# FFN1 of two token blocks and two feature tiles by seven block products instead of eight, in a transformer block on one core

## The chip, the core and the metric

The kernel runs on one core of one Trainium2 chip. The metric is the device time of one execution in microseconds; before the change it is 1167.24 us, the median of 3 runs from 1166.67 to 1168.52. Engine names are those of the profile: PE multiplies matrices, DVE (vector) and ACT (scalar) work element by element, POOL does odd jobs, and SP issues nearly all transfers.

## The reference

One layer in which attention and a feed-forward network (FFN) read the same normalized input and both are added to it. There are 2048 tokens (S), width 576 (D), 32 heads of 18, and FFN width 4608 (F).

```python
xn = _layernorm(x, axis=-1)
return x + _A_ref(xn, A_wqkv, A_wo) + _B_ref(xn, B_w1, B_b1, B_w2, B_b2)
...
h = jnp.einsum("bsd,df->bsf", x, w1) + b1
r = jnp.where(h > zero, h, zero)
h = r * r
out = jnp.einsum("bsf,fd->bsd", h, w2) + b2
```

Attention is local: each token looks at itself and at 7 earlier ones, 2 apart.

## The kernel before

The tokens lie in four blocks (b) of 512, the FFN width in 36 tiles (f) of 128, and the 576 rows of width in 4 chunks of 128 and one of 64. Every fp32 operand is split into a high part (the fp32r rounding, written by ACT) and a rest (a subtraction on DVE), and a product is high x high + high x rest + rest x high. In the last chunk the 64 rows are doubled, so that high and rest share one matmul. So a step of FFN1 (`ffn1`, L448) takes 14 matmuls of 512 columns into one PSUM tile `wk`: 5 of high x high, 4 of the weights' high with `xl`, 5 of the weights' rest. Then ACT does relu with bias out of PSUM into `r`, and squares it twice, into the rounded `hh` and in place; DVE makes `hl`, the rest. FFN2 (`ffn2`, L486) of the step takes 14 matmuls more, onto five PSUM tiles `y` that stay open through a block.

The program walks through 4 x 36 = 144 such steps, `step(n)` at L618. Each step loads a tile of w1 (320 KB) and of w2 (288 KB), splits w1 for the next step (`split_w1`, one copy on ACT, one subtraction on DVE, 640 wide) and w2 for its own, and runs FFN2 two steps late (`LAG`). Between them stand, by a table of step numbers, the QKV projections of a block (4 groups of 8 heads, each 4 row tiles of 14 matmuls of 432 columns, `qkv_rows`), the attention of the groups on DVE, cut into pieces that a step takes three of (`piece`), the layernorm of the next block, and the output projection onto the same `y` tiles (`o_chunk`, `o_acc`). Only the first QKV group's order is written by hand (`open_rows`); else a scheduler sets each engine's order from the program's order and its own estimate of when things are ready. An engine then works through its list in that order.

In attention, DVE multiplies q with 8 shifted keys (`pr`, 1152 wide), sums up (`lg`), takes the softmax with one exponential on ACT, multiplies with the values and adds in three halvings, for each of 4 rows of queries. Keys and values of a group go to DRAM (`kscr`, `vscr`) and come back with the 14 tokens before them.

Of the kernel before, what the change touches and what calls it, by code (L numbers as in the profile page):

```python
# [2 lines left out]

# [17 lines left out]
NB = S // TB  # L21
NJ = TB // P
NC = 5
NF = F // P
G = 4
# [10 lines left out]
LAG = 2  # L36
WARM = 11
WQ, KV = 448, 2688
# [3 lines left out]
def block_kernel(ctx: ExitStack, tc: tile.TileContext, x, xt, wqkv, wo, w1, b1, w2, b2, out):  # L42
    nc = tc.nc
    const = ctx.enter_context(tc.tile_pool(name="const", bufs=1))
    mt = ctx.enter_context(tc.tile_pool(name="mt", bufs=1))
# [23 lines left out]
    nc.vector.tensor_reduce(out=flip[:, 0:1], in_=ident.rearrange("p (g f) -> p g f", g=G)[:, :, L // 2:],  # L69
                            axis=AX.XY, op=ALU.add)  # L70
    nc.vector.tensor_scalar(out=flip[:, 1:2], in0=flip[:, 0:1], scalar1=-2.0, scalar2=1.0, op0=ALU.mult, op1=ALU.add)
# [4 lines left out]
    vscr = [dram.tile([PAD + S, CG], F32, name=f"vscr{g}") for g in range(G)]  # L76

# [3 lines left out]

    oscr = {(b, g): dram.tile([TB, CG], F32, name=f"o{b}{g}") for b in range(NB) for g in range(G)}
    mrscr = {b: dram.tile([P, 2 * NJ], F32, name=f"mr{b}") for b in range(1, NB)}

    normed, mb = {0}, {}
    xb, xT, xr, xh, xl, qo, ob, wq = {}, {}, {}, {}, {}, {}, {}, {}
    raw1, raw2, w1s, w2s, hs = {}, {}, {}, {}, {}
    yp = {}

    def load_x(b):  # L90
        xb[b] = sb.tile([P, NJ, D], F32, name="xb", bufs=1)
        with tc.issue_after(last_load[0].ins):
            nc.sync.dma_start(xb[b], xv[b])
            xT[b] = sb.tile([P, NC, TB], F32, name="xt", bufs=1)
            nc.sync.dma_start(xT[b], xt[b])

    def load_first():
        xb[0] = sb.tile([P, NJ, D], F32, name="xb", bufs=1)
        raw = sb.tile([P, NC, TB], F32, name="xr", bufs=1)[:, :, :3 * CG]
        hi = mt.tile([P, NC, WQ], F32R, name="wqh")[:, :, :3 * CG]  # L100
        lo = mt.tile([P, NC, WQ], F32R, name="wql")[:, :, :3 * CG]
        nc.sync.dma_start(xb[0][:64, 0], xv[0, :64, 0])
        nc.scalar.dma_start(xb[0][64:, 0], xv[0, 64:, 0])
        nc.scalar.dma_start(raw[:, 0], wqkv[0, :, 0])
        nc.sync.dma_start(xb[0][:, 1], xv[0, :, 1])
        for c in range(1, NC):
            nc.sync.dma_start(raw[:, c], wqkv[0, :, c])
        for j in range(2, NJ):
            nc.sync.dma_start(xb[0][:, j], xv[0, :, j])
        for scr in (kscr[0], vscr[0]):  # L110
            nc.sync.dma_start(scr[:PAD], zero)
        return raw, hi, lo

    def split(hi, lo, raw, only=None):
        if only is not nc.vector:
            i = nc.scalar.activation(hi, raw, AF.Copy)  # L116
        if only is not nc.scalar:
            i = nc.vector.tensor_tensor(out=lo, in0=raw, in1=hi.bitcast(F32), op=ALU.subtract)  # L118
        return i

    def split_out(w, raw):
        nc.scalar.activation(w[:, :D], raw, AF.Copy)  # L122
        for o, a, n in ((NC * P, 0, DM), (D, DM, D - DM)):
            nc.vector.tensor_tensor(out=w[:, o:o + n], in0=raw[:, a:a + n], in1=w[:, a:a + n].bitcast(F32),  # L124
                                    op=ALU.subtract)

    ln, last_load, last_hl = {}, [None], [None]

    def open_x(b):
        xh[b] = mt.tile([P, NC, TB], F32R, name="xh", bufs=2)  # L130
        xl[b] = mt.tile([P, NC - 1, TB], F32R, name="xl", bufs=2)

    def bn_stats(b, j, k):
        if k == 0:
            ln[b, j] = sb.tile([P, 2, 6], F32, name="st", bufs=NJ)
        nc.vector.bn_stats(out=ln[b, j][:, k], in_=xb[b][:, j, k * 288:(k + 1) * 288])  # L136

    def mean_var(b, j):
        mv = sb.tile([P, 2], F32, name="mv", bufs=NJ)
        nc.vector.bn_aggr(out=mv, in_=ln[b, j])  # L140
        ln[b, j] = mv

    def inverse_std(rs, var):
        nc.vector.tensor_scalar(out=rs, in0=var, scalar1=EPS, scalar2=None, op0=ALU.add)  # L144
        nc.gpsimd.tensor_tensor(out=rs, in0=rs, in1=half, op=ALU.pow)  # L145

    def row_scale(j):
        mean_var(0, j)
        rs = sb.tile([P, 1], F32, name="rs", bufs=NJ)
        inverse_std(rs, ln[0, j][:, 1:2])  # L150
        return rs

    def minus_mean(j, rs):
        nm = sb.tile([P, 1], F32, name="nm", bufs=2)
        nc.vector.tensor_scalar(out=nm, in0=ln[0, j][:, 0:1], scalar1=-1.0, scalar2=rs, op0=ALU.mult, op1=ALU.mult)
        return nm

    def normalize_rows(xn, j, rs, on_act, nm=None):
        mv = ln[0, j]
        if on_act:  # L160
            nc.scalar.activation(xn[:, j, :D], xb[0][:, j], AF.Identity, bias=nm, scale=rs)
        else:
            nc.vector.tensor_scalar(out=xn[:, j, :D], in0=xb[0][:, j], scalar1=mv[:, 0:1], scalar2=rs,  # L163
                                    op0=ALU.subtract, op1=ALU.mult)
        nc.gpsimd.tensor_copy(xn[:, j, D:], xn[:, j, DM:D])

    def turn(y, xn, j, cs):
        for i, c in enumerate(cs):
            nc.tensor.transpose(y[:, i * P:(i + 1) * P], xn[:, j, c * P:(c + 1) * P], ident)  # L169

    def take(y, j, cs):
        js = slice(j * P, (j + 1) * P)
        if cs[0] < NC - 1:
            v = y[:, :len(cs) * P].rearrange("p (c t) -> p c t", c=len(cs))
            hi, lo = xh[0][:, cs[0]:cs[-1] + 1, js], xl[0][:, cs[0]:cs[-1] + 1, js]
            nc.scalar.activation(hi, v, AF.Copy)  # L176
            nc.vector.tensor_tensor(out=lo, in0=v, in1=hi.bitcast(F32), op=ALU.subtract)
        else:
            t = sb.tile([P, TB], F32R, name="r", bufs=3)[:, :P]
            hi = xh[0][:, NC - 1, js]  # L180
            nc.scalar.activation(t[64:], y[64:, :P], AF.Copy)
            nc.scalar.activation(hi[:64], y[:64, :P], AF.Copy)
            nc.vector.tensor_tensor(out=hi[64:], in0=y[64:, :P], in1=t[64:].bitcast(F32), op=ALU.subtract)

    def open_rows():
        xn = sb.tile([P, NJ, NC * P], F32, name="xt", bufs=1)
        open_x(0)
        y = open_y()
        raw, hi, lo = first_wq
        rs = {}  # L190

        def w_hi(c):
            nc.scalar.activation(hi[:, c], raw[:, c], AF.Copy)

        def w_lo(c, eng):
            eng.tensor_tensor(out=lo[:, c], in0=raw[:, c], in1=hi[:, c].bitcast(F32), op=ALU.subtract)  # L196

        def stats(j):
            for k in range(2):
                bn_stats(0, j, k)  # L200
            rs[j] = row_scale(j)
# [9 lines left out]
        def part(j, i):  # L211
            hi, lo = qw[0]
            a, c = divmod(i, 10)
            js = slice(j * P, (j + 1) * P)
            if (0, j) not in qp:
                qp[0, j] = pw.tile([P, TB], F32, name="wk")
                done[j] = 0
            done[j] += 1
            nc.tensor.matmul(qp[0, j][:, :3 * CG], (xl if a == 1 else xh)[0][:, c, js], (lo if a == 2 else hi)[:, c],  # L219
# [6 lines left out]
        done = {}  # L226
# [3 lines left out]
        normalize_rows(xn, 0, rs[0], False)  # L230
# [6 lines left out]
        nm = minus_mean(1, rs[1])  # L237
# [5 lines left out]
        normalize_rows(xn, 1, rs[1], True, nm)  # L243
        qkv_open(0, 0, (hi, lo))
# [5 lines left out]
        bn_stats(0, 2, 0)  # L250
        take(y[2], 0, (4,))
        bn_stats(0, 2, 1)
        rs[2] = row_scale(2)
# [5 lines left out]
        normalize_rows(xn, 2, rs[2], False)  # L259
        stats(3)  # L260
        nm = minus_mean(3, rs[3])
# [4 lines left out]
        qkv_out(0, 0, 0)  # L266
        normalize_rows(xn, 3, rs[3], True, nm)
        parts(1, 13, 4, 24)
        qkv_out(0, 0, 1)
# [3 lines left out]
        split_w1(0)  # L273
        parts(2, 12, 13, 4, 24)
        qkv_out(0, 0, 2)
        parts(3, 0, 1, 2, 3, 20, 21, 22, 23, 10, 11, 12, 13, 4, 24)
        split_w1(1)
        last_act = qkv_out(0, 0, 3)
        ffn1(0)
        qkv_close(0, 0)  # L280
        return last_act

    def layernorm(b):
        mr = sb.tile([P, 2, NJ], F32, name="mr", bufs=1)
        for j in range(NJ):
            for k in range(2):
                bn_stats(b, j, k)
            mean_var(b, j)
            nc.vector.tensor_copy(mr[:, 0, j:j + 1], ln[b, j][:, 0:1])
            inverse_std(mr[:, 1, j:j + 1], ln[b, j][:, 1:2])  # L290
            yield
        n = 2 * NJ
        nc.sync.dma_start(mrscr[b], mr.rearrange("p k j -> p (k j)"))
        mb[b] = sb.tile([P, P, 2, NJ], F32, name="mb", bufs=1)
        nc.sync.dma_start(mb[b].rearrange("c p k j -> c (p k j)"), flat(mrscr[b], 0, [0, P], n * P))

    def normalize(b):
        open_x(b)
        for c in range(NC):
            with tc.issue_after(last_hl[0].ins):  # L300
                for k, op in enumerate((ALU.subtract, ALU.mult)):
                    v = xT[b][:, c].rearrange("c (j p) -> c j p", j=NJ)
# [382 lines left out]
```

## Time and profile before

| | |
|---|---|
| median of 3 runs | 1167.24 us |
| span of the profiled execution | 1165.5 us |
| PE busy | 1157.4 us, 99% |
| DVE busy | 846.0 us, 73% |
| ACT busy | 602.0 us, 52% |
| granted clock of PE, mean | 0.998 |
| DMA | 185.90 MB, mean 160 GB/s |
| FFN1 matmuls (L460) | 2016 |
| FFN2 and projection matmuls (L483) | 2276 |

The span runs from the first to the last instruction of the profiled execution; the page gives it no other time. In a group's row stand the source line, the engine, what is written from what, the shape and the count; behind the bar the busy time of the group and the mean length of one in ns, and behind the second bar the engine's idle time just before such instructions with what ended it. Lengths of neighbours on an engine overlap a little. A matmul's length contains its way through the array; what counts is the distance between two. The chain of waits goes back from the last instruction to what released each; its pieces are given with start, length and count.

### The profile page before, as it was taken

What the parts mean: (1) busy time and instruction counts of PE and PEld (TensorE: products, weight loads), DVE (VectorE), ACT (ScalarE), POOL (GpSimd) and SP (SyncE); (2) the same over time, 40 slices, a digit from 0 to 9 for tenths busy, and PEclk for the clock granted to TensorE, in tenths of its full rate; (3) what the DMA queues carried; (4) which work ended last, traced back from release to release, by engine and by line L of the source; (5) the groups of instructions that cost most, each with busy time, mean ns of one, the idle gap of its engine ahead of it and who ended that gap; (6) DMA issues with size and microseconds to landing.
All of it is one profiled execution on the core that took longest, in us unless ns stands there. A gap on an engine that the chain in (4) does not pass through costs nothing.

```text
span 1165.5 us, 14768 instructions
## 1 busy us (share of the span) xinstructions
PE 1157.4 (99%) x5219; PEld 978.5 (84%) x5219; DVE 846.0 (73%) x1366; ACT 602.0 (52%) x1083; POOL 19.9 (2%) x33
## 2 busy tenths in 40 slices
PE   8999999999999999999999999999999999999998
PEld 6888888888888888888888888888888888888886
DVE  6868698892788686985287959698529795857452
ACT  6645445563545454555364545455535455445542
POOL 2001000000000100000000010000000000000000
PEclk9999999999999999999999999999999999999999
DMA  7656446332666556333266664534336745343321
GB/s 254 231 179 228 148 158 217 115 117 74 205 209 192 210 187 202 119 114 120 63 233 231 213 196 138 201 114 127 106 91 223 229 128 189 115 164 114 113 62 51
DMA packets 89114, 185.90 MB, mean 160 GB/s; under 512 B 9936, under 2 KB 36688, under 8 KB 87760
## 3 DMA queue, kind: packets, MB, share of 16 engines
q1 hardware_dynamic: 88816, 184.59, 48.6%
q8 instruction: 41, 0.67, 0.2%
q10 hardware_dynamic: 224, 0.37, 0.1%
q14 instruction: 33, 0.27, 0.1%
HBM read 165.96 MB, written 18.96 MB: 159 GB/s over the span
## 4 chain that ended last, share of the span: by engine, by line
PE 99%; DMA 0%; DVE 0%; POOL 0%; issue 0%; ACT 0%; POOLq 0%; DVEq 0%
PE y L483 44%; PE wk L460 39%; PE wk L340 14%; PE wk L219 1%; DMA xb<-in_x 0%; PE y L169 0%; DVE xt L163 0%; DVE st L136 0%; DVE xr L498 0%; POOL rs L145 0%; ACT xh L176 0%; DVE mv L140 0%; DVE rs L144 0%; DVEq L136 0%; POOLq L196 0%
## 5 line engine op out<-in xcount | busy, mean ns | idle before, releaser
L483 PE MATMUL y<-hh,w2s 128*128 128x512 f32 x1296 | 320.7, 389 | 0.0
L483 PEld LDWEIGHTS y<-hh,w2s 128*128 128x128 f32 x1296 | 243.3, 188 | 50.5
L460 PE MATMUL wk<-xh,w1h 128*128 128x512 f32 x720 | 210.2, 389 | 0.0
L483 PE MATMUL y<-hl,w2s 128*128 128x512 f32 x720 | 190.0, 389 | 0.0
L460 PE MATMUL wk<-xh,w1l 128*128 128x512 f32 x720 | 186.6, 389 | 0.0
L116 ACT ACTIVATE w1h<-raw 128x640 fp32r<-128x640 f32 x144 | 106.1, 737 | 118.0 <-PE wk L460 114.8
L118 DVE TENSOR_TENSOR w1l<-raw,w1h 128x640 fp32r<-128x640 f32 x144 | 117.9, 819 | 63.2 <-ACT w1h L116 46.1
L122 ACT ACTIVATE w2s<-raw 128x576 fp32r<-128x576 f32 x144 | 97.9, 683 | 119.8 <-PE y L483 119.0
L460 PEld LDWEIGHTS wk<-xh,w1l 128*128 128x128 f32 x720 | 135.2, 188 | 28.1
L483 PEld LDWEIGHTS y<-hl,w2s 128*128 128x128 f32 x720 | 135.2, 188 | 28.1
L460 PEld LDWEIGHTS wk<-xh,w1h 128*128 128x128 f32 x720 | 135.2, 188 | 27.0
L460 PE MATMUL wk<-xl,w1h 128*128 128x512 f32 x576 | 154.0, 389 | 0.0
L124 DVE TENSOR_TENSOR w2s<-raw,w2s 128x512 fp32r<-128x512 f32 (+1 forms) x288 | 118.1, 452 | 44.9 <-ACT w2s L122 43.9
L467 DVE TENSOR_TENSOR hl<-r,hh 128x512 fp32r<-128x512 f32 x144 | 98.7, 686 | 49.9 <-ACT r L466 49.9
L460 PEld LDWEIGHTS wk<-xl,w1h 128*128 128x128 f32 x576 | 108.1, 188 | 22.5
L462 ACT ACTIVATE r<-wk,b1t 128x512 f32<-128x512 f32 x144 | 98.5, 684 | 42.7 <-PE wk L460 42.5
L393 DVE TENSOR_TENSOR pr<-qo,kv 128x1152 f32<-128x1152 f32 x64 | 86.5, 1352 | 37.4 <-DMA kv<-kscr 37.4
L340 PE MATMUL wk<-wqh,xh 128*128 128x432 f32 x300 | 107.4, 358 | 0.0
L340 PE MATMUL wk<-wql,xh 128*128 128x432 f32 x300 | 107.4, 358 | 0.0
L466 ACT ACTIVATE r<-r 128x512 f32<-128x512 f32 x144 | 91.2, 633 | 4.4
L465 ACT ACTIVATE hh<-r 128x512 fp32r<-128x512 f32 x144 | 90.9, 632 | 4.3
L415 DVE TENSOR_TENSOR pr<-lg,kv 128x1152 f32<-128x1152 f32 x64 | 86.8, 1356 | 1.4
(83 smaller groups left out, 960.5 us busy)
## 6 DMA issues: line engine op xcount, KB each, us to landing
raw<-in_w SPq DMA_DIRECT2D x144, 320.0 KB, 3.1
raw<-in_w SPq DMA_DIRECT2D x144, 288.0 KB, 2.8
wqr<-in_wqkv SPq DMA_DIRECT2D x75, 216.0 KB, 3.4
kv<-kscr SPq DMA_DIRECT2D x16, 1008.0 KB, 5.8
kv<-vscr SPq DMA_DIRECT2D x16, 1008.0 KB, 8.4
raw<-in_wo SPq DMA_DIRECT2D x20, 288.0 KB, 2.7
kscr<-kv SPq DMA_DIRECT2D x16, 288.0 KB, 2.7
vscr<-kv SPq DMA_DIRECT2D x16, 288.0 KB, 3.2
```

The lines of the kernel that those rows point to most:

```text
L116: i = nc.scalar.activation(hi, raw, AF.Copy)
L118: i = nc.vector.tensor_tensor(out=lo, in0=raw, in1=hi.bitcast(F32), op=ALU.subtract)
L122: nc.scalar.activation(w[:, :D], raw, AF.Copy)
L124: nc.vector.tensor_tensor(out=w[:, o:o + n], in0=raw[:, a:a + n], in1=w[:, a:a + n].bitcast(F32), op=ALU.subtract)
L340: nc.tensor.matmul(ps, l, r, start=i == 0, stop=i == len(mm) - 1)
L415: nc.vector.tensor_tensor(out=pr.rearrange("p w (a d) -> p w a d", d=DH), in0=at[:, :, :, None].to_broadcast([P, W, HG, DH]), in1=shifted( ...
L460: nc.tensor.matmul(p, l, r, start=i == 0, stop=i == len(mm) - 1)
L462: nc.scalar.activation(r, p, AF.Relu, bias=b1t[:, f:f + 1])
L465: nc.scalar.activation(hh, r, AF.Square)
L466: nc.scalar.activation(r, r, AF.Square)
L467: last_hl[0] = nc.vector.tensor_tensor(out=hl, in0=r, in1=hh.bitcast(F32), op=ALU.subtract)
L483: nc.tensor.matmul(yp[b][c], v, a, start=first and c not in cs[:i], stop=last and c not in cs[i + 1:], skip_group_check=True)
```

## The change

The four blocks become two superblocks (s) of 1024 tokens, and the 36 feature tiles 18 pairs (q). For each of the 36 (s, q), a `quad` computes two feature tiles for two token blocks at once. The 512 full rows of width are halved, which makes the product a 2 x 2 by 2 x 2 block product; it is done by seven block products instead of eight, with sums of blocks prepared on both sides (Strassen's scheme in Winograd's form). A block product takes 6 matmuls of 512 columns: 2 chunks, each high x high, high x rest and rest x high. The last chunk of 64 rows goes on top of four of the products, 2 matmuls each. On the token side, `combine_x` prepares the sums `th`, `tl` once per superblock; on the weight side, `split_w1` makes four sums of 128x256 on DVE per quad and splits 2048 columns in two halves on ACT and DVE. Three PSUM tiles serve a quad, X, Y and V. X gathers products and is copied out three times between them by ACT (`snap`, with the bias); DVE adds these copies to Y and V (three adds of 128x512 out of PSUM per quad), and ACT takes the relu.

A superblock is done in two phases. In phase A, the quads run for both blocks; the relu of the first block (`r1`) is squared at once and goes to FFN2, one quad late, put into the quad's two gaps (`fill(0)`, `fill(1)`); the relu of the second block (`r2`) goes to DRAM (`rscr`, 512 KB a quad). In phase B it is loaded again, one q ahead, squared, and FFN2 of the second block runs; w2 is loaded and split again, as before once per block. Phase B of the first superblock also holds the QKV of the second's two blocks.

The start changes too: after the first QKV group, written by hand as before, all the other QKV groups of blocks 0 and 1 come first, and FFN1 starts after them. q goes through DRAM as keys and values do (`qscr`), and one wide copy on ACT per row tile replaces three. Attention is one stream over all 16 (block, group) that is drawn upon whenever the sum of DVE costs falls under 0.93 of PE's, both counted by a `Meter` from sizes as instructions are written. The buffers are fewer: w1 splits take 4 of 2048 columns, which the QKV weights share; raw w2 has 2 buffers for 3; and `r1`, `r2`, loaded relus, QKV results, residuals and projection inputs share 5 tiles of 1024 columns (`pair_tile`). As all calls go through `Meter`, most instructions of PE and DVE have line 57 in the changed kernel.

```diff
-    def ffn1(n):
-        b, f = divmod(n, NF)
-        hi, lo = w1s.pop(n)
-        p = pw.tile([P, TB], F32, name="wk")
...
-        for i, (l, r) in enumerate(mm):
-            nc.tensor.matmul(p, l, r, start=i == 0, stop=i == len(mm) - 1)
...
+    def split_w1(n):
+        r = raw1.pop(n)
+        hi = mt.tile([P, 2048], F32R, name="w1h", tag="w1", bufs=4)
+        lo = mt.tile([P, 2048], F32R, name="w1l", tag="w1", bufs=4)
+        part = lambda i: r[:, i * K2:(i + 1) * K2]
+        copy_hi(hi[:, :1024], r[:, K2:1280])
+        rest(lo[:, :1024], r[:, K2:1280], hi[:, :1024])
+        a21, a11, a12, a22 = (part(i) for i in range(4))
+        s1, s2, s3, s4 = (part(5 + i) for i in range(4))
+        vec.tensor_tensor(out=s1, in0=a21, in1=a22, op=ALU.add)
+        sub(s2, s1, a11)
+        sub(s3, a11, a21)
+        sub(s4, a12, s2)
+        copy_hi(hi[:, 1024:], r[:, 1280:])
+        rest(lo[:, 1024:], r[:, 1280:], hi[:, 1024:])
...
+    def squares(key, r):
+        hh = mt.tile([P, 2, TB], F32R, name="hh", bufs=2)
+        hl = mt.tile([P, 2, TB], F32R, name="hl", bufs=2)
+        nc.scalar.activation(hh, r, AF.Square)
+        nc.scalar.activation(r, r, AF.Square)
+        rest(hl, r, hh)
...
+        def product(p, i, first, extra=None):
+            o, bh, bl = ops[i]
+            mm = []
+            for k in range(2):
+                w = slice(o * K2 + k * P, o * K2 + (k + 1) * P)
+                mm += [(hi[:, w], bh[:, k]), (hi[:, w], bl[:, k]), (lo[:, w], bh[:, k])]
+            if extra is not None:
+                f, t = extra
+                w = slice(3 * K2 + f * P, 3 * K2 + (f + 1) * P)
+                mm += [(hi[:, w], xe[s][:, t]), (lo[:, w], xe[s][:, t])]
+            for j, (l, r) in enumerate(mm):
+                ten.matmul(p, l, r, start=first and j == 0, stop=j == len(mm) - 1, skip_group_check=True)
...
+        product(X, 1, True)
+        p1 = snap(X, 0)
...
+        product(Y, 2, True, (0, 0))
+        product(X, 6, False)
+        u2 = snap(X, 1)
+        add(r1[:, 0], Y, p1)
...
+        product(V, 7, True, (1, 1))
+        relu(r1[:, 0])
+        product(X, 5, False)
+        u4 = snap(X, 1)
+        add(r2[:, 1], V, u4)
+        fill(0)
+        relu(r2[:, 1])
+        product(X, 3, False, (0, 1))
+        nc.scalar.activation(r2[:, 0], X, AF.Relu, bias=bias[0])
+        nc.sync.dma_start(rscr[s, q], r2)
+        product(V, 4, False, (1, 2))
+        add(r1[:, 1], V, u2)
+        relu(r1[:, 1])
+        fill(1)
+        squares((b0, q), r1)
...
+    def load_r(s, q):
+        rp[s, q] = pair_tile("rs")
+        nc.sync.dma_start(rp[s, q], rscr[s, q])
...
+            squares((b, q), rp.pop((s, q)))
```

The order of PE in the middle of a superblock's work, FFN1 and FFN2 of block 0, where `wk` is FFN1's PSUM tile and `y` FFN2's. Before:

```order
L460 MATMUL wk<-xh,w1h 128x512 x4
L460 MATMUL wk<-xl,w1h 128x512 x4
L460 MATMUL wk<-xh,w1h 128x512
L460 MATMUL wk<-xh,w1l 128x512 x5
L483 MATMUL y_475<-hh,w2s 128x512
```

In the changed kernel, in the middle of phase A, a product of `th` with its tail of the last chunk (`xe`), and FFN2 behind it:

```order
L57 MATMUL wk<-th,w1h 128x512
L57 MATMUL wk<-tl,w1h 128x512
L57 MATMUL wk<-th,w1l 128x512
L57 MATMUL wk<-th,w1h 128x512
L57 MATMUL wk<-tl,w1h 128x512
L57 MATMUL wk<-th,w1l 128x512
L57 MATMUL wk<-xe,w1h 128x512
L57 MATMUL wk<-xe,w1l 128x512
L57 MATMUL y_1336<-hl,w2s 128x512
```

The 14 matmuls of a step in one run have become products of 6 or 8, and FFN2 stands between products.

The order of PE where the first QKV group ends. Before, FFN1 follows:

```order
L219 MATMUL wk<-wqh,xl 128x432 x4
L219 MATMUL wk<-wqh,xh 128x432
L219 MATMUL wk<-wql,xh 128x432
L460 MATMUL wk<-xh,w1h 128x512 x4
L460 MATMUL wk<-xl,w1h 128x512 x4
```

In the changed kernel, the next QKV group with newly split weights `wqh`, `wql` follows:

```order
L57 MATMUL wk<-wqh,xl 128x432 x4
L57 MATMUL wk<-wqh,xe 128x432
L57 MATMUL wk<-wql,xe 128x432
L57 MATMUL wk<-wqh,xh 128x432 x3
L57 MATMUL wk<-wql,xh 128x432
L57 MATMUL wk<-wqh,xl 128x432
```

The order of DVE among attention's instructions (`pr`, `lg`), with FFN's `hl` and the splits `w1l`, `w2s`. Before:

```order
L393 TENSOR_TENSOR pr<-qo,kv 128x1152
L467 TENSOR_TENSOR hl<-r,hh 128x512
L396 TENSOR_REDUCE lg<-pr 128x8x8
L124 TENSOR_TENSOR w2s<-raw_2642,w2s 128x512
L124 TENSOR_TENSOR w2s<-raw_2642,w2s 128x64
L393 TENSOR_TENSOR pr<-qo,kv 128x1152
L118 TENSOR_TENSOR w1l<-raw_2851,w1h 128x640
```

In the changed kernel, in the first phase A; `r_2658` and `r_2818` are `r1` of two quads that follow each other:

```order
L57 TENSOR_TENSOR pr<-q,k 128x1152
L57 TENSOR_TENSOR wos<-rwo,wos 128x512
L57 TENSOR_TENSOR wos<-rwo,wos 128x64
L57 TENSOR_TENSOR r_2658<-wk,snap 128x512
L57 TENSOR_REDUCE lg<-pr 128x8x8
L57 TENSOR_TENSOR w1l<-raw_2642,w1h 128x1024 x2
L57 TENSOR_TENSOR r_2818<-wk,snap 128x512
L57 TENSOR_TENSOR pr<-q,k 128x1152
L57 TENSOR_TENSOR hl<-r_2658,hh 128x1024
```

The adds out of PSUM, on which PE's next use of the tile waits, now stand in DVE's row between attention's instructions and the splits.

More of the change, by code (lines that the diff above doesn't have):

```diff
@@ L97, in load_first, with pair_tile @@
-    def load_first():
[L98 to L103, printed above, removed]
+    def pair_tile(name="rp"):
+        return mt.tile([P, 2, TB], F32, name=name, tag="r", bufs=5)
@@ new lines, in accumulate, with open_y @@
+    def accumulate(b, a_hi, a_lo, w, first, last, only=None):
+        ops = [o for o in w2_ops(a_hi, a_lo, w) if only in (None, o[0])]
+        cs = [o[0] for o in ops]
+        for i, (c, v, a) in enumerate(ops):
+            ten.matmul(yp[b][c], v, a, start=first and c not in cs[:i],
+                             stop=last and c not in cs[i + 1:], skip_group_check=True)
+    def open_y():
+        return [py.tile([P, TB], F32, name=f"y{i}") for i in range(NC)]
+    def squares(key, r):
[4 more added lines that the diff above has]
+        rest(hl, r, hh)
+        hs[key] = hh, hl
@@ L147, in row_scale @@
[L147 to L165, printed above, removed]
+        return rows, raw
@@ L642, in block_kernel @@
-    for n in range(NT + 1):
-        with opening() if n < 7 else ExitStack():
-            step(n)
+        nc.sync.dma_start(b1t, b1)
+        nc.sync.dma_start(b2t, b2)
+        side += [layernorm(1)]
+        for i, rows_of in enumerate(qkv_pass(0, (1, 2, 3), (1,), take_some)):
+            rows_of()
+            if i == 2:
+                drain_all(side)
+                load_xt(1)
+                side += [normalize(1)]
+            work(side)
+        drain_all(side)
+        spare[2:] = []
```

940 lines of the change are left out of this document (554 added, 386 removed).

## The prediction

> **What bounds the kernel now.** First the page's busy line, then its chain by engine, then the table of busy time by stage.
>
> ```profile
> PE 1157.4 (99%) x5219; PEld 978.5 (84%) x5219; DVE 846.0 (73%) x1366; ACT 602.0 (52%) x1083; POOL 19.9 (2%) x33
> PE 99%; DMA 0%; DVE 0%; POOL 0%; issue 0%; ACT 0%; POOLq 0%; DVEq 0%
> 0.00:30.00 30.00, 26.17 (x116) 20.35 (x117) 19.25 (x45) 19.31 (x46) 8.30 (x21) 0.94 0.77 258
> 300.00:600.00 300.00, 300.00 (x1355) 254.25 (x1354) 223.61 (x356) 156.20 (x281) 4.27 (x4) 1.00 0.51 169
> 600.00:900.00 300.00, 300.00 (x1355) 254.18 (x1355) 224.96 (x361) 156.64 (x279) 4.27 (x4) 1.00 0.50 163
> ```
>
> PE (first number after the stage's length) is busy 300.00 of 300.00 us at clock 1.00; DVE (third) stands at 75%. A busy PE need not be a full PE, so the chain's pieces give the pace, and its groups the counts.
>
> ```profile
> 23.57 8.43 PE wk L460 x37
> 74.38 10.97 PE wk L340 x56
> 1121.10 6.35 PE y L483 x28
> 1161.26 0.75 DVE L498 SCALAR_TENSOR_TENSOR xr<-y,b2t,xr 128x512 f32<-128x512 f32 x1 [0.29 <-PE y L483]
> L483 PE MATMUL y<-hh,w2s 128*128 128x512 f32 x1296 | 320.7, 389 | 0.0
> L483 PE MATMUL y<-hl,w2s 128*128 128x512 f32 x720 | 190.0, 389 | 0.0
> L483 PE MATMUL y<-kv,wos 128*128 128x512 f32 x260 | 62.8, 389 | 0.0
> L460 PE MATMUL wk<-xh,w1h 128*128 128x512 f32 x720 | 210.2, 389 | 0.0
> L460 PE MATMUL wk<-xh,w1l 128*128 128x512 f32 x720 | 186.6, 389 | 0.0
> L460 PE MATMUL wk<-xl,w1h 128*128 128x512 f32 x576 | 154.0, 389 | 0.0
> L340 PE MATMUL wk<-wqh,xh 128*128 128x432 f32 x300 | 107.4, 358 | 0.0
> L340 PE MATMUL wk<-wql,xh 128*128 128x432 f32 x300 | 107.4, 358 | 0.0
> L340 PE MATMUL wk<-wqh,xl 128*128 128x432 f32 x240 | 85.9, 358 | 0.0
> ```
>
> A 512-column matmul takes 6.35/28 = 0.2268 us, a 432-column one 10.97/56 = 0.1959. FFN1 has 720 + 720 + 576 = 2016, FFN2 and the output projection 1296 + 720 + 260 = 2276, QKV behind the opening 840. From 23.57: 23.57 + 840 x 0.1959 + 4292 x 0.2268 = 1161.5; the last drain starts at 1161.26. So PE has no gap at all after the opening, and every matmul taken out is worth 0.2268 us. Behind the last matmul lie 1165.5 - 1161.2 = 4.3 us. The span is 1.7 us under the median of 1167.2.
>
> **The matmuls.** A quad replaces 2 x 2 FFN1 steps of 14 matmuls, 56, by seven products of 6 and four tails of 2, 50. There are 36 quads: 1800 for 2016, 216 fewer, 216 x 0.2268 = 49.0 us. The order of PE keeps the counts of FFN2, projection and QKV. The stream alone then ends at 23.57 + 164.6 + 4076 x 0.2268 = 1112.6, the span at 1116.9, the median at 1118.6.
>
> [...]
>
> **What DVE gets.** Lengths of one instruction, with the releaser of idle time at the end of some rows:
>
> ```profile
> L118 DVE TENSOR_TENSOR w1l<-raw,w1h 128x640 fp32r<-128x640 f32 x144 | 117.9, 819 | 63.2 <-ACT w1h L116 46.1 <-PE wk L460 16.5 <-issue 0.3
> L467 DVE TENSOR_TENSOR hl<-r,hh 128x512 fp32r<-128x512 f32 x144 | 98.7, 686 | 49.9 <-ACT r L466 49.9
> L124 DVE TENSOR_TENSOR w2s<-raw,w2s 128x512 fp32r<-128x512 f32 x144 | 98.7, 686 | 44.9 <-ACT w2s L122 43.9
> L124 DVE TENSOR_TENSOR w2s<-raw,w2s 128x64 fp32r<-128x64 f32 x144 | 31.3, 218 | 0.0
> L415 DVE TENSOR_TENSOR pr<-lg,kv 128x1152 f32<-128x1152 f32 x64 | 86.8, 1356 | 1.4
> L393 DVE TENSOR_TENSOR pr<-qo,kv 128x1152 f32<-128x1152 f32 x64 | 86.5, 1352 | 37.4 <-DMA kv<-kscr 37.4
> L396 DVE TENSOR_REDUCE lg<-pr 128x64 f32<-128x1152 f32 x64 | 86.2, 1346 | 0.0
> L404 DVE TENSOR_TENSOR lg<-lg,mx 128x256 f32<-128x256 f32 x16 | 6.7, 419 | 0.2
> L501 DVE TENSOR_TENSOR xr<-y,xr 64x512 f32<-64x512 f32 x4 | 2.8, 694 | 0.1
> ```
>
> 512 and 1152 columns give 1.04 ns a column and 153 ns fixed, so 1024 columns take 1.22 us. Per quad: split of w1 2 x 1.22 + 4 x 0.419 = 4.11; three adds out of PSUM 3 x 0.694 = 2.08; hl 1.22; two w2 splits 2 x 0.904 = 1.81; together 9.2. Phase B repeats hl and w2: 3.0. That is 12.2 where four steps before took 4 x (0.819 + 0.686 + 0.904) = 9.6: 2.6 more per quad, 94 us in all. All of the changed kernel's DVE rows at such lengths come to 1014; before's come to 910 where the page has 846, since neighbours overlap. At that ratio, 0.93, DVE is busy 943 us, 84% of 1118. ACT falls: a 128x640 w1 copy per step becomes 2048 columns per quad for 2560.
>
> The mean hides the stages. One phase A quad is (50 + 28) x 0.2268 = 17.7 us of PE. From the first hl to the eighteenth, PE has 17 x 17.7 + 65 projection matmuls x 0.2268 = 315.5. DVE's order there holds 483 instructions, 340 us by length, of which 144 are attention (a (block, group) of it sums to 24.3) and 28 are rows of the next superblock's normalization that fill in; times 0.93, 316 with the filling and 290 without. In the second phase A, from the start to the eleventh hl, 224 x 0.93 = 208 against 209. So DVE has no room there beyond 25 us of work that nobody waits for. Phase B is easy: 200 x 0.93 = 185 us of DVE against 217 of PE, then 73 x 0.93 = 68 against 129.
>
> **Where PE may now wait.** ACT's lengths, and the loads that each stage needs:
>
> ```profile
> L116 ACT ACTIVATE w1h<-raw 128x640 fp32r<-128x640 f32 x144 | 106.1, 737 | 118.0 <-PE wk L460 114.8 <-DVE hl L467 1.4 <-DVE pr L393 1.4
> L462 ACT ACTIVATE r<-wk,b1t 128x512 f32<-128x512 f32 x144 | 98.5, 684 | 42.7 <-PE wk L460 42.5
> L466 ACT ACTIVATE r<-r 128x512 f32<-128x512 f32 x144 | 91.2, 633 | 4.4
> L116 ACT ACTIVATE wqh<-wqr 128x432 fp32r<-128x432 f32 x75 | 40.5, 561 | 84.7 <-DMA wqr<-in_wqkv 55.2 <-PE wk L340 29.2
> raw<-in_w SPq DMA_DIRECT2D x144, 288.0 KB, 2.8
> mb<-mr SPq DMA_DIRECT2D x3, 512.0 KB, 4.1
> kv<-vscr SPq DMA_DIRECT2D x16, 1008.0 KB, 8.4
> ```
>
> (1) Opening. FFN1 steps with ready weights follow the first QKV group today; now the next QKV group does, and its split stands on ACT behind the copy of the last row tile: about 0.6 + 0.56, then the matmuls run slower than the split. Between 0 and 4, taken 1.5.
>
> (2) Block 1's QKV starts 12 row tiles later, at 23.6 + 1.5 + 12 x 14 x 0.196 = 58, and needs xl of block 1. DVE's order has 55 us of lengths up to xl's second half, 51 at the ratio 0.93, and DVE idles 30 - 19.25 = 10.8 us of the first 30 today: 51 + 10.8 = 62. In that order eight attention instructions and three w2 splits stand ahead of the normalization. The reload of the statistics costs 4.1 by the row of mb, behind a store now made of 4-byte pieces. Between 0 and 10, taken 4.
>
> (3) The first quad has no FFN2 to cover its V: X's third product (8 x 0.227 = 1.8) covers snap and add (0.684 + 0.694) and little more. 0 to 3, taken 1.
>
> (4) A to B, twice: behind the last product stand add, relu, two squares of 1024 columns (about 1.05 each) and hl: 0.69 + 0.63 + 2.1 + 1.22 = 4.6 and five hand-overs; FFN2's 14 matmuls cover 3.2. Taken 2 each, 4; 0 to 8.
>
> (5) Adds, snaps and splits inside the other quads. Covers are 1.8 us for each snap and 14 to 34 matmuls (3.2 to 7.7) for the adds; an attention instruction ahead on DVE costs 1.35. With 25 us of slack DVE should hold. Taken 2; 0 to 15.
>
> The DRAM trip of the second block is hidden: a 512 KB load, 4.1 by mb's row, one FFN2 pair (28 x 0.2268 = 6.35) ahead; uncovered it would cost 4.1 once per phase. In bytes a phase B pair asks for 512 + 2 x 288 KB in 6.35 us, 175 GB/s, plus the next QKV; the first 30 us ran at 258. SP issues 36 stores and 36 loads more and 108 w1 loads fewer; POOL keeps its rows. Sum: 1.5 + 4 + 1 + 4 + 2 = 12.5; 1118.6 + 12.5 = 1131.1.
>
> **The rivals.** *DVE becomes the bound of phase A.* For: 316 of 315.5. Today each of 16 attentions waits 37.4/16 = 2.3 for its keys; if six and four such waits and an exponential's 0.4 each come unfilled, and the filling isn't put off, A loses 16 + 11 us: 1158. Against: 28 us can slip, and k is now loaded one half ahead.
>
> *The quad's serial chain, slower than before.* X is copied twice in mid-accumulation before PE may write on. Snap waits in ACT's order behind a relu that waits for a DVE add, itself behind two attention instructions: 2 x 1.35 + 0.694 + 0.684 - 1.8 = 2.3 us where it happens, against 1.1 (38/36) per quad from which the change loses. If every second of the 72 snaps in mid-accumulation meets it, 36 x 2.3 = 83: 1118.6 + 10.5 + 83 = 1212; if every third, 24 x 2.3 = 55: 1184. Against: PE's order pulls the next quad's first product in between.
>
> *Phase B starves.* raw2 has two buffers now, three before: split 0.68 + 0.90 and load 2.8 fit into 3.2 x 2 us, but at the 8.4 of vscr's load they don't: about 1 us in each of the 28 pairs without QKV, 1159.
>
> *Gaps cool the clock.* Row 0 to 30 has clock 0.94: 1.8 us lost beside its gaps. Five gaps at the hand-overs would cost 5 x 1.8: 1140. [...]
>
> That the change does not do what it says is excluded by the order: 1800.
>
> **How the numbers follow.** Forecast 0.68, DVE 0.12, chain 0.07, phase B 0.08, clock 0.05. All but the chain are faster; 0.2% is 2.3 us, which a measurement of this kernel just tells from none. Faster 0.91, same 0.02, slower 0.07. Low: no wait at all, 1118.6, less 1.6 for the run-to-run spread, 1117. High: the five terms' ends add to 40, 1159; not all meet, so 1158, where DVE's rival lies. The tails beyond hold the chain and half of phase B.
>
> **What would show it.** Right: 36 x 50 FFN1 matmuls at 0.227, PE idle near 12 us in the opening and at A to B, DVE near 940. Wrong: PE idle spread over the quads, released by DVE's adds (first rival) or ACT's snaps (second), by w2s in phase B, or a clock under 1.00 after 60 us; or a 512-column matmul that isn't 0.227.

## The result, and the profile after

The changed kernel takes 1185.08 us (median of 4 runs, 1179.87 to 1188.41), the one before 1167.49 (4 runs, 1166.67 to 1168.52): a ratio of 1.0145, 95% interval 1.0119 to 1.0172. It is slower, by 17.6 us, where 36 us less were forecast. The profiled execution took 1188.41, with a span of 1186.7; it is the longest of the four, so its losses below are some 3 us above those of the median.

From the changed kernel's page, the busy line, the chain by engine and the packets:

```profile
PE 1134.6 (96%) x5003; PEld 948.8 (80%) x5003; DVE 922.0 (78%) x1458; ACT 584.0 (49%) x837; POOL 17.6 (1%) x33
PE 66%; DVE 16%; DMA 13%; issue 2%; ACT 2%; SPq 1%; POOL 0%; DVEq 0%; ACTq 0%; POOLq 0%
DMA packets 88918, 214.46 MB, mean 181 GB/s; under 512 B 13072, under 2 KB 36752, under 8 KB 84368
```

The 216 matmuls are gone (5003 for 5219), and DVE is at 922 us, under the 943 forecast. But the chain, 99% PE before, now has 29% of DVE and DMA in it. The table by stage says where. After a stage's length come the busy time in us and the instructions of PE, PEld, DVE, ACT and POOL, then the granted clock, the share of DMA and its GB/s:

```profile
30.00:75.00 45.00, 38.61 (x183) 35.87 (x182) 33.05 (x49) 16.87 (x29) 1.07 (x2) 0.92 0.94 251
75.00:140.00 65.00, 62.64 (x301) 56.16 (x300) 58.90 (x88) 30.94 (x50) 0.00 (x0) 1.00 0.53 178
140.00:225.00 85.00, 85.00 (x376) 70.38 (x376) 79.97 (x122) 46.95 (x64) 0.00 (x0) 1.00 0.52 181
225.00:300.00 75.00, 64.33 (x261) 51.64 (x261) 54.72 (x112) 31.92 (x45) 6.25 (x8) 0.91 0.64 143
300.00:420.00 120.00, 119.56 (x528) 98.66 (x527) 113.48 (x178) 63.10 (x89) 0.00 (x0) 1.00 0.53 175
420.00:520.00 100.00, 93.39 (x405) 76.39 (x404) 86.84 (x126) 56.87 (x80) 0.00 (x0) 0.98 0.67 225
520.00:1005.00 485.00, 483.44 (x2184) 409.79 (x2184) 396.50 (x606) 243.58 (x348) 0.00 (x0) 1.00 0.54 180
1005.00:1100.00 95.00, 80.82 (x311) 64.08 (x310) 39.80 (x66) 37.49 (x48) 0.00 (x0) 0.89 0.43 140
```

In the middle of phase A (140 to 225) PE does 376 matmuls in 85.00 us, 0.226 each: the stream is as forecast. Most of the loss sits in four places: 30 to 75, 225 to 300, 420 to 520 and 1005 to 1100. In the last, 95 us would hold 419 matmuls; 311 are done, 108 or 24.5 us fewer. PE is idle for 95 - 80.82 = 14.2 of that; the other 10 are matmuls at a clock of 0.89. In this trace the granted clock is 1 or 0.5 and never between; a stretch at 0.5 is called a spell below.

The same for the whole trace: from each matmul's start to the next, less 0.2268 (0.1959 for 432 columns), distances over by more than 0.3 us counted as waits, the rest as slow matmuls. (A matmul's length in the rows of before, 389 ns for 512 columns and 358 for 432, is 162 ns over its distance in both.)

| place, us | term of the forecast | waits | slow matmuls |
|---|---|---|---|
| 24 | (1), 1.5 | 1.4 | |
| 30 to 75 | (2), 4 | 7.0 | 2.6 |
| 75 to 140 | (3), 1 | 2.7 | 0.4 |
| 225 to 300 | none | 11.5 | 4.6 |
| 420 to 520 | (4), 2 | 7.6 | 2.5 |
| 300 to 420, 520 to 1005 | (5), 2 | 2.5 | 0.5 |
| 1005 to 1030 | (4), 2 | 2.0 | 1.7 |
| 1030 to 1100 | none | 13.9 | 7.1 |

Together 68.0; the span less the gapless one is 1186.7 - 1116.9 = 69.8, and the 1.8 left over lie in the opening.

What PE waited for, the four largest rows of the table of waits (total, times, longest):

```profile
PE y L57 <- ACT wos L115: 12.9, 6, 4.5
PE wk L57 <- DVE r L57: 9.5, 4, 4.2
PE y L57 <- DVE hl L57: 6.4, 2, 6.2
PE wk L57 <- ACT qkv L249: 6.4, 2, 5.0
```

No row says that DVE is the bound of a whole phase, and ACT's `snap` has 1.1 us in two waits. The wait of 5.0 us in the last row begins at 54 us. ACT stood for 11.5 us at the split of w2, until its load landed at 58, with QKV's copies queued behind it. The DMA view of 40 to 58 us (slices of 0.45 us, busy tenths and GB/s; then loads, KB and us to landing):

```profile
DMA  9998699999999929999199536359687999979999
GB/s 438 438 392 276 205 348 394 410 371 382 292 170 182 231 10 20 20 13 10 3 10 15 5 10 10 10 20 44 31 46 54 161 261 300 310 295 392 390 366 256
wqr<-in_wqkv SPq DMA_DIRECT2D x1, 432.0 KB, 12.2
raw<-in_w SPq DMA_DIRECT2D x1, 288.0 KB, 11.0
```

From the fifteenth slice on, for 7.6 us, the queues move 3 to 54 GB/s, and yet are busy for more than half of the time. Under way is the 4 KB store of block 1's statistics, in 1024 pieces of 4 bytes, issued at 36 and landed 19.1 us later. The w2 load issued meanwhile takes 11.0 us, where the median before was 2.8. The page counts 13072 packets under 512 B for 9936 before, 3136 more; three stores of 1024 pieces, where there were 128 pieces each, are 2688 of them. The two other stores, issued at 239 and 265, lie in front of the waits that begin at 246 and 277.

The waits from 1030 on are another thing. The chain there:

```profile
1041.89 0.69 ACT wos L115
1042.63 9.00 PE y L57 x28
1051.65 0.70 ACT w2s L115
1052.37 3.54 DMA rwo<-in_wo
1055.99 0.69 ACT wos L115
1056.73 8.27 PE y L57 x28
```

A ring: the split of w2 frees a raw buffer, only then wo is loaded into it, split, and used; its split tile frees the next. The output projection's `rwo` and `wos` share the two raw and three split tiles of w2 (`o_chunk`).

At the entry of phase B (466 us) PE waits 3.43 us for the last quad's add, which stands in DVE's order behind this:

```profile
464.69 0.82 DVE L57 TENSOR_TENSOR w2s<-raw,w2s 128x512 fp32r<-128x512 f32 x2
465.43 1.22 DVE L57 TENSOR_TENSOR xraw<-xraw 128x1024 f32<-128x1024 f32 x1
466.57 1.35 DVE L57 TENSOR_TENSOR pr<-lg,v 128x1152 f32<-128x1152 f32 x1
467.84 1.22 DVE L57 TENSOR_TENSOR xraw<-xraw 128x1024 f32<-128x1024 f32 x1
468.97 0.68 DVE L57 TENSOR_TENSOR r<-wk,snap 128x512 f32<-128x512 f32 x1
```

For 30 us around this hand-over DVE (third) has hardly a gap:

```profile
450.00:480.00 30.00, 25.34 (x107) 20.80 (x106) 29.94 (x41) 17.71 (x28) 0.00 (x0) 0.94 0.64 214
```

So there were four theories: (1) the 4-byte store jams the queues; (2) the projection's ring of shared tiles; (3) the normalization of the next superblock, ahead of the last quad's add; (4) a wait of PE brings a spell. The rival to the first three is that DVE, or the two raw buffers alone, make the waits.

### The profile page after: what moved, and what is told of

It reads as the page before. It is cut to its first block, busy times and chain, and to the rows that moved or that the text cites. A ratio compares the mean times of both kernels' runs of the same rounds, so it can differ in the third digit from the quotient of the medians.

```text
span 1186.7 us, 14078 instructions
## 1 busy us (share of the span) xinstructions
PE 1134.6 (96%) x5003; PEld 948.8 (80%) x5003; DVE 922.0 (78%) x1458; ACT 584.0 (49%) x837; POOL 17.6 (1%) x33
## 2 busy tenths in 40 slices
DMA packets 88918, 214.46 MB, mean 181 GB/s; under 512 B 13072, under 2 KB 36752, under 8 KB 84368
## 4 chain that ended last, share of the span: by engine, by line
PE 66%; DVE 16%; DMA 13%; issue 2%; ACT 2%; SPq 1%; POOL 0%; DVEq 0%; ACTq 0%; POOLq 0%
PE y L57 35%; PE wk L57 31%; DMA raw<-in_w 4%; DVE pr L57 3%; DMA rwo<-in_wo 2%; DVE xraw L57 2%; DVE lg L57 1%; DMA wqr<-in_wqkv 1%; DVE wql L57 1%; DMA o<-q 1%; DVE hl L57 1%; DMA xb<-in_x 1%; DVE w2s L57 1%; DMA mr<-mr 1%; DMA kscr<-qkv 1%
## 5 line engine op out<-in xcount | busy, mean ns | idle before, releaser
L57 PE MATMUL wk<-th,w1h 128*128 128x512 f32 x288 | 112.5, 391 | 4.5 <-DVE r L57 4.5
L57 PE MATMUL wk<-tl,w1h 128*128 128x512 f32 x288 | 112.5, 391 | 0.0
L57 PE MATMUL wk<-th,w1l 128*128 128x512 f32 x288 | 112.2, 390 | 0.0
L57 DVE TENSOR_TENSOR r<-wk,snap 128x512 f32<-128x512 f32 x108 | 73.8, 683 | 42.6 <-PE wk L57 25.7
L57 PE MATMUL wk<-wqh,xl 128*128 128x432 f32 x256 | 92.4, 366 | 0.0
L57 DVE TENSOR_TENSOR pr<-q,k 128x1152 f32<-128x1152 f32 x64 | 86.5, 1352 | 2.3 <-DMA k<-kscr 1.6
L57 DVE TENSOR_TENSOR pr<-lg,v 128x1152 f32<-128x1152 f32 x64 | 86.6, 1353 | 0.9
L57 DVE TENSOR_TENSOR w1l<-raw,w1h 128x1024 fp32r<-128x1024 f32 x72 | 86.6, 1217 | 0.9 <-ACT w1h L115 0.9
L57 PE MATMUL wk<-xh,w1h 128*128 128x512 f32 x216 | 84.4, 391 | 2.7 <-DVE r L57 1.6
L57 DVE TENSOR_REDUCE lg<-pr 128x64 f32<-128x1152 f32 x64 | 86.2, 1348 | 0.5
L57 PE MATMUL y<-oh,wos 128*128 128x512 f32 x260 | 72.4, 424 | 13.9 <-ACT wos L115 12.9
```

The source lines that it names most:

```text
L57: return f(*args, **kw)
```

## The experiments

All are edits of the changed kernel but the fourth, which edits the kernel before. The third joins the first and the second, the sixth the fifth and the second; the seventh builds on the sixth, the ninth on the seventh, the tenth on the ninth. Ratios are to the kernel before. The scheduler sets the orders anew for each kernel. By the traces, the fourth has the order of the kernel before on every engine, and the second and the eighth have that of the changed kernel up to 1009 us; in the first, the fifth, the seventh, the ninth and the tenth other instructions moved too, so there the edit is not the only difference.

**The store in 32-byte pieces.** The layout of before, one piece per partition, read with a stride:

```diff
-        nc.sync.dma_start(mrscr[b].rearrange("n p -> p n"), mr.rearrange("p k j -> p (k j)"))
+        nc.sync.dma_start(mrscr[b], mr.rearrange("p k j -> p (k j)"))
...
+                    vec.tensor_tensor(out=u, in0=u, in1=rows[:, k], op=op)
```

> Edit: the changed kernel, in which alone the store of the layernorm statistics goes back to one piece of 32 bytes per partition (as before the change), and the normalization reads them with a stride instead. Theory 1 (the 3 stores of 1024 pieces of 4 bytes jam the queues: the w2 and w1 loads issued meanwhile take 10 to 15 us): the store lands within 4 us, the waits of PE at 54, 67, 246 and 277 us and the half-clock spells behind them go (5.3 + 1.7 + 2.3 and 16 us), and the time comes to 1160 (1155 to 1167). Rival (DVE at its limit, or the two raw buffers of w2 by themselves make these waits): the waits stay, 1185 +- 4.

Measured: 1181.5 us, 1.0121 (1.0101 to 1.014). A miss of 21.5 us, and the store of block 1 still took 9.7 us to land where 4 were expected. The stage tables show the theory at work in one place: at 225 to 300 the loss falls from 16.1 to 3.7. At 30 to 75 it is 8.4 for 9.6, and at 420 to 520 it grows from 10.1 to 22.9:

```profile
225.00:300.00 75.00, 73.13 (x316) 60.02 (x316) 67.58 (x131) 39.39 (x55) 7.86 (x8) 0.98 0.55 175
420.00:520.00 100.00, 86.31 (x348) 69.81 (x347) 82.38 (x119) 51.06 (x72) 0.00 (x0) 0.91 0.57 184
```

The edit had a price of its own. This kernel's normalization reads its statistics 8 words apart; below it is a contiguous row of twice the columns (min, median, max ns), and then the same step in the kernel before the change, where it was read so too:

```profile
L57 DVE TENSOR_TENSOR xraw<-xraw,mb x24: 1056/1129/1203, 53.7 to 445.3; 128x512 f32<-128x512 f32 x24
L57 DVE TENSOR_TENSOR xraw<-xraw x8: 1160/1220/1252, 64.9 to 462.9; 128x1024 f32<-128x1024 f32 x8
```

```profile
L303 DVE TENSOR_TENSOR xt<-xt,mb x30: 1122/1147/1183, 233.7 to 803.3; 128x512 f32<-128x512 f32 x30
```

1.129 us where half of 1.220 would do: 24 x 0.52 = 12 us more on DVE, 16 of the 24 (8 us) between 420 and 446, ahead of the hand-over at which DVE is full. So the edit changed two things, and it shows what transposing the statistics had bought.

**Own tiles for the last projection.** In the last block `th` and `w1` are idle:

```diff
+        else:
+            r = mt.tile([P, 2 * TB], F32, name="rwo", tag="th", bufs=4)[:, :D]
+            w = mt.tile([P, 2048], F32R, name="wos", tag="w1", bufs=4)[:, :2 * D]
```

> Edit: the changed kernel, in which alone the output projection of the last block gets other buffers: raw wo from the idle th tiles (4) and the split wo from the idle w1 tiles (4), instead of sharing 2 raw buffers and 3 split buffers with w2. Theory 2 (load, split and use of wo and w2 stand in one serial ring): the six waits of 2.2 to 4.8 us between 1020 and 1095 us and the half-clock spells behind them go, 18 to 25 us, and the time comes to 1163 (1159 to 1168). Rival (the load itself, or DVE's transposes of the attention output, is what comes late): the waits stay and the time is 1185 +- 4.

Measured: 1167.46 us, 1.0004 (0.9992 to 1.0016), 17.6 less. All but one of the waits go:

```profile
1005.00:1100.00 95.00, 92.97 (x402) 76.03 (x401) 47.30 (x82) 46.06 (x61) 0.00 (x0) 0.98 0.56 176
```

402 matmuls for 311, and the loss is 4.2 for 24.7. Theory 2 stands: nothing moved ahead of 1009 us, and the five waits on `wos` are gone. The wait of 2.2 us at the start of the stage, the second hand-over from A to B, stays.

This run, with the eighth, also tells how far a stage differs between two profiles of one order. At 75 to 140 us, where the changed kernel has 301 matmuls, the second and the eighth have:

```profile
75.00:140.00 65.00, 59.49 (x277) 53.31 (x276) 54.41 (x80) 28.47 (x47) 0.00 (x0) 0.95 0.51 168
75.00:140.00 65.00, 64.22 (x310) 57.92 (x309) 59.08 (x87) 31.87 (x51) 0.00 (x0) 1.00 0.53 178
```

The loss there is 3.1, 8.5 and 1.1 us with no edit near: one wait for a quad's add is 1.6 us, 4.7 or none.

**Both.**

> Edit: both edits of the first two experiments at once. If the two causes stand apart in time and share nothing, the gains add: 1138 (1132 to 1146), with PE's waits left at the entry of phase B of the first superblock (10 us with cold matmuls), in the opening and at the first quads. If instead DVE is the bound behind them, time gained in one place is lost in another: 1155 or more.

Measured: 1163.5 us, 0.9956 (0.9933 to 0.9978). The two gains were 3.6 and 17.6, together 21.2; 21.6 came. They add as far as these 7 runs, from 1157.5 to 1168.0, can tell, but with one gain of 3.6 that is a weak test; the miss is that of the first experiment.

**The store alone, in the kernel before.** The other way round:

```diff
-        nc.sync.dma_start(mrscr[b], mr.rearrange("p k j -> p (k j)"))
+        nc.sync.dma_start(mrscr[b].rearrange("n p -> p n"), mr.rearrange("p k j -> p (k j)"))
```

> Edit: the kernel before the change, in which alone the statistics are stored transposed, in 4-byte pieces, as in the changed kernel. Theory 1: the store's landing grows from 1.4 to 12 us or more each time, and the loads issued in that time take about 11 us for 3; with three raw buffers and no shared ring PE loses between 0 and 15 us, so 1167 to 1182. Rival (the piece size is harmless and the store was slow in the changed kernel because of what else was queued): it lands within 5 us and the time is 1167 +- 2.

Measured: 1182.08 us, 1.0123 (1.0108 to 1.0138): 14.7 us lost by three stores of 4 KB, with the order of every engine as before, with another FFN1, other buffers and DVE at 73%, and although the normalization gets its contiguous rows. The time is at the end of the range; the stores landed after 9.4, 10.4 and 8.8 us, for 2.8, 1.4 and 1.4 before, where 12 or more were expected. Its DMA view from 88 to 108 us (slices of 0.5 us), and what PE waits for:

```profile
DMA  1000979899999959562959236357039799999989
GB/s 61 20 0 0 138 226 406 336 369 239 281 126 114 32 81 97 32 48 16 65 16 65 16 16 32 16 32 65 0 97 339 300 409 395 439 374 487 453 356 432
raw<-in_w SPq DMA_DIRECT2D x1, 320.0 KB, 13.9
raw<-in_w SPq DMA_DIRECT2D x1, 288.0 KB, 10.2
mr<-mr SPq DMA_DIRECT2D x1, 4.0 KB, 9.4
```

```profile
PE wk L460 <- DVE w1l L118: 7.7, 3, 3.1
PE wk L460 <- ACT w1h L116: 3.7, 2, 2.2
```

For 8 us the queues carry 97 GB/s at most, a load of w1 takes 13.9, and PE waits 1.7 us for its split at 106.

The other two stores, at 394 and 689, cost more, and in another way. SP issues in order, and the reload of the statistics waits for their store to land. Behind the reload stand the loads of the next attention, of QKV's weights and of w1. SP's wait there (total, times, longest), in the kernel before and in this run, and the DMA view of 689 to 697 us (slices of 0.2 us):

```profile
SPq L295 <- DMA mr<-mr: 2.0, 2, 1.0
SPq L295 <- DMA mr<-mr: 24.7, 3, 10.0
```

```profile
DMA  0001776000000000000000000000000000000000
GB/s 0 0 0 1 7 7 6 0 0 0 0 0 0 0 0 0 0 0 0 0 0 0 0 0 0 0 0 0 0 0 0 0 0 0 0 0 0 0 0 0
mr<-mr SPq DMA_DIRECT2D x1, 4.0 KB, 8.8
```

Nothing else is under way: the pieces pass within 0.8 us, and the store lands 7 us later, at 697.6. Only then are the reload and all behind it issued: the load of w1 is issued 21.1 us behind the store, 11.9 before. PE's other four waits, 9.7 of the 11.4 us, begin at 417, 421, 711 and 716. So late landing is shown to be the cause in this kernel; that it jams other loads is seen at the first store alone.

**The store in 128-byte pieces, read contiguously.** The clean form of the first:

```diff
+        vec.transpose(turned, rows8)
+        for i in range(P // L):
+            nc.sync.dma_start(mrscr[b][:, i * L:(i + 1) * L], turned[i * L:i * L + 2 * NJ])
```

> Edit: the changed kernel, in which alone the statistics are turned on DVE (one 32x32-block transpose of 128x32, about 0.15 us) and stored in 128-byte pieces; the normalization reads them as in the changed kernel, 1024 columns at once. Reason: the first experiment's strided reading made a 512-column subtraction or product take 1.06 to 1.12 us where half of a 1024-column one takes 0.61, which adds some 11 us to DVE, so it changed two things. Theory 1 alone: the loss at 225 to 300 us falls from 16 to 1 to 4 us as there, and the entry of the first phase B stays at 10 us instead of 23: 1170 (1166 to 1175). Rival (the entry becomes dearer whenever the statistics come earlier): 1178 or more.

Measured: 1170.35 us, 1.0018 (1.0001 to 1.0034), 14.7 less, as expected. The turning took 0.205 us; the 0.15 was the author's estimate. The stages:

```profile
225.00:300.00 75.00, 74.88 (x329) 61.39 (x328) 71.65 (x137) 40.62 (x56) 6.00 (x8) 1.00 0.55 180
420.00:520.00 100.00, 91.66 (x403) 74.67 (x402) 78.98 (x125) 59.70 (x83) 0.00 (x0) 1.00 0.64 204
```

The loss at 225 to 300 is 0.7 for 16.1, at 30 to 75 it is 6.4 for 9.6; at 420 to 520 it stays (11.0). Theory 1 stands for the price of the store. That it is 14.7 us here and in the kernel before is chance: here two of the three stores have no reload waiting behind them (the reloads come at 433 and 440), and the cost is slow loads; there it is mostly SP's wait.

**Turned, and own tiles.**

> Edit: the last one and the own buffers for the last block's output projection together. Gains of separate places add: 1152 (1147 to 1157). If DVE is a common bound behind both: 1160 or more.

Measured: 1149.09 us, 0.9849 (0.9834 to 0.9863), 36.0 less than the changed kernel; the two gains alone are 14.7 + 17.6 = 32.3. The 3.7 more are within the noise of the four times; a DVE that took back what these edits gain (1160 or more) is ruled out.

**Block 3's statistics later.** Two `xr`, two `mb` and `r1` are five tiles of tag `r`, which has five, so the last quad's `r2` has to wait for one. This is theory 3 by way of the tiles:

```diff
                 load_xt(b + 2)
-                load_xt(b + 3)
...
+            if more and q == 0:
+                load_xt(b + 2)
```

> Edit: as the last one, and the transposed x and the statistics of block 3 are loaded in the first step of phase B instead of ahead of the last quad of phase A. Theory 3: two residuals, two mb and r1 fill the five tiles of tag r, so r2 of the last quad has to wait until the normalization of block 2 has let go of its mb; with one mb less the add doesn't wait, and of the 10 us that PE loses at 420 to 520 us some 6 go: 1146 (1142 to 1150). Rival: DVE is simply full there (98% busy), the tiles play no part, and nothing changes, 1152 +- 2.

Measured: 1145.14 us, 0.981 (0.9794 to 0.9825), 4.0 less. The time fits, the place only in part: at 420 to 520 the loss falls from 10.5 to 7.7. The wait for the add, 2.6 us, is gone, and PE now waits there for `w2s` instead. So theory 3 explains 2.8 of 10.5 us at most; as the scheduler also moved other instructions from 424 us on, that the tiles alone did it is not shown.

**Waits filled with matmuls.** Nobody reads their result:

```diff
+                    for i in range(14):
+                        ten.matmul(p, hh[:, 0, :P], hl[:, 0], start=True, stop=True)
                 o_acc(b, q - o_at - 1)
```

> Edit: the changed kernel with 14 matmuls of 512 columns, whose result nobody reads, ahead of each of the five chunks of the last block's output projection (5 x 14 x 0.2268 = 15.9 us of PE in the place of 15.9 us of waits). Theory 4 (a wait of over about 2 us brings a spell of half clock behind it, whatever PE waits for): the 8.8 us of slow matmuls between 1005 and 1100 us go, the waits are filled instead of cut, and where a filling is longer than its wait some us are lost again: 1178 (1174 to 1182), mean granted clock of that stage above 0.97 instead of 0.90. Rival (the clock falls for another reason, or the waits are after the added matmuls): 1185 to 1201.

Measured: 1182.1 us, 1.0125 (1.0109 to 1.014), 3.0 less than the changed kernel with 70 matmuls more. That is just outside the range, and the interval overlaps the changed kernel's, so the gain in time is not shown; the clock is.

```profile
1005.00:1100.00 95.00, 91.33 (x401) 74.65 (x400) 40.65 (x69) 39.82 (x51) 0.00 (x0) 1.00 0.48 147
```

The clock is 1.00 for 0.89, slow matmuls cost 0.4 us for 8.8. Waits fall by 11.8 where 15.9 of filling was put in: 4.1 more against 8.4 less, 4.3 gained in this stage of the profile. So the clock falls because PE waits. But not every wait brings a spell: in the same run PE waits 3.4 us for the add at the first hand-over, and the clock of 460 to 475 us is 1.00.

**w2's split behind QKV's copies, and a later normalization.** First ACT's split of w2 in the first phase A is queued behind the last QKV copy:

```diff
+            with tc.issue_after(copied[0].ins):
+                for i in range(2):
+                    split_w2(b * NF + 2 * q + i)
```

> Edit: as the last best kernel (statistics turned, own buffers for the projection, block 3's statistics later), and the split of w2 in phase A of the first superblock is queued on ACT behind the last QKV copy. Theory: ACT's split of w2 for the first quad waits 8 us for its load with QKV's copies queued behind it, and the loss of PE at 50 to 75 us (2.4) goes: 1143 (1140 to 1147). Rival (the loss is set by DVE's normalization of block 1, which comes as late): 1145 +- 2.

Then the preparation of block 2 is also queued behind the last quad's add and relu:

```diff
+                    with tc.issue_after(tail[0].ins), tc.issue_after(tail[1].ins):
+                        work(prep)
```

> Edit: as the one before, and the normalization of block 2 and the split of its first QKV weights are queued on DVE and ACT behind the last add and relu of the last quad of phase A. If normalization that is pulled ahead of the add still delays the entry of phase B, the loss at 420 to 520 us falls from 7.7 to 4: 1140 (1136 to 1144). Rival (DVE has the same work to do in the same stage, so a later normalization makes QKV late instead): 1143 to 1150.

Measured: 1143.21 us, 0.9783 (0.9767 to 0.98), and 1148.07 us, 0.9837 (0.982 to 0.9853). Two stages of the first, and the later of them in the second:

```profile
100.00:140.00 40.00, 34.33 (x142) 28.10 (x141) 33.18 (x52) 18.13 (x27) 0.00 (x0) 0.91 0.50 165
420.00:520.00 100.00, 95.45 (x421) 77.80 (x420) 85.02 (x129) 60.88 (x85) 0.00 (x0) 1.00 0.64 212
```

```profile
420.00:520.00 100.00, 91.95 (x387) 75.98 (x386) 80.23 (x121) 56.85 (x80) 0.00 (x0) 0.91 0.62 203
```

The first is the fastest here, 2.2% under the kernel before. But its interval touches that of the one it is built on, and its time fits its rival (1145 +- 2) as well, so the theory is left open. The opening loses 2.2 for 3.2 at 30 to 75 and the first quads 9.0 for 3.9 at 100 to 140; the latter is again the wait for a quad's add, 4.9 us here, which runs of one order had at 4.7 us or not at all. The second fell to its rival: with the normalization held back the loss at 420 to 520 is 14.7, not 4. DVE and ACT have that work to do in that stage, and the fixed place tried here is worse than the scheduler's.

## Why the prediction was wrong

The forecast was 1131.1, the time is 54.0 us longer. Two costs that the sum did not hold, the store's late landing and the last projection's ring, are 36.0 of that together (sixth experiment).

*The gain* was right: 216 matmuls at 0.2268, and a stream without gaps wherever nothing waits. Terms (1) and (5), 1.4 and 3.0 for 1.5 and 2, and the chain rival came out as reasoned; no quad of 140 to 225 us waits at all, with DVE busy 79.97 of 85 us.

*Term (2) failed in its step on the statistics.* It says "behind a store now made of 4-byte pieces" and prices the reload at 4.1 by `mb`'s row. The store itself got no price, and only block 1 was asked about. It lands after up to 19.1 us, and the loads beside it are late: 14.7 us over three blocks (fifth experiment). Two of the three stores lie at 225 to 300, where the sum had no term at all and the loss was 16.1. In the term's own stage the loss of 9.6 was inside its 0 to 10, and 6.4 of it stay without the 4-byte pieces.

*The ring had no term, and the rival nearest to it, on raw2's two buffers, had it in the wrong place.* The rival priced about 1 us in each of the 28 pairs without QKV for w2 itself; after 520 us PE never waits for a split of w2. It left out who else draws on the tag: `rwo`, and `wos` on the split tiles. Five chunks with waits of 2 to 4.5 us and the spells behind them made 21 us in the profile; 17.6 of the time went with the second experiment.

*Term (4)* took 2 us each, with a bound of 8 for both. The stage of the first lost 10.1, that of the second 3.7. The working added up the chain of the last product's results, but not what DVE has queued ahead of it (normalization, splits) when a phase ends. The prediction's sum on DVE had 25 us of slack over all of phase A, from work that nobody waits for; at its end that work is waited for, by QKV, and DVE is busy 29.94 of 30.00 us. That is the DVE rival in one place, and that DVE's work sets the loss there is argued: the first experiment put 8 us more of it there and the loss was 12.8 more, but no run took work away. The seventh lowered the loss by 2.8, the tenth raised it by 7.3 over the ninth.

*Term (3)* was 3.1 for 1.

*The clock* was a rival, at five gaps of 1.8, where it belonged into every term: in the trace, from 8 us on, there are 21.3 us of slow matmuls beside 49.6 of waits, 0.4 for each. In the kernel before, PE stands idle for 2.54 us up to 7.83, and its clock is 0.50 from 7.7 to 11.1: that one spell is the 0.94 of the opening. In the changed kernel's trace, spells up to 1100 us last 3.4, 6.8 or 10.2 us; in the tenth experiment the clock over 420 to 520 us is 0.91. How long a wait has to be to bring one is not shown: the wait for `hh` at the second hand-over, 1.8 us by its releaser in both, did in the changed kernel (clock 0.87 from 1018 to 1031) and did not in the eighth experiment (1.00 from 1005 to 1100).

*What stays open.* The fastest version still is 24.6 us over the forecast's gapless 1118.6: in its profile 9.0 at the first quads, 7.4 at 420 to 520, 3.9 in the opening. Why one and the same order waits at the first quads in some runs and not in others, whether less work on DVE at 420 to 520 would end that loss, and what holds a store of 4-byte pieces for 7 us after the last piece has passed, was not tried.

## What to carry to other kernels

Price a store by its pieces, by the loads beside it and by what the issuing engine holds back until it lands, not by its bytes: the same 4 KB landed after 1.4 to 2.8 us in 32-byte pieces and after 8.8 to 10.4 in 4-byte ones (fourth experiment). Where tiles share a tag, write down everyone who draws on it, stage by stage; a ring of load, split and use that fits for one user doesn't for two (17.6 us, second experiment). And add something for the clock to the waits of a full PE: over whole traces here 0.2 (eighth experiment) to 0.4 us for each us of waiting, while a single wait of 1.8 to 3.4 us brought either nothing or a spell. Before a stage's loss is put down to an edit, look how much it differs between two profiles of one order: here up to 7 us.

## What the hardware showed beside that

The statistics' reading, 8 words apart, cost DVE 1.129 us for 512 columns, where half of a contiguous step of 1024 is 0.61 (first experiment); the kernel before paid 1.147 us for it, 30 times, where it was hidden. Turning 128x32 on DVE took 0.205 us (fifth experiment), so contiguous reading and 128-byte pieces are both to be had.

1024 pieces of 4 bytes pass a free queue within 0.8 us, and their store lands 7 us later (fourth experiment, 689 us); around the landing of the first store, the loads beside it carry 97 GB/s at most for 8 us (94.5 to 102.5 us there). So in the store at 689 us it is not the passing of the pieces that takes the time.
